# Norm with an operand in PSUM, x by transposes, two expert steps moved ahead, part of the w2 split on GpSimd

## The chip, the cores and the metric

The kernel runs on 1 core of one Trainium2 chip. The metric is the device time of one execution in microseconds (us), lower is better. Of the kernel before there are three timed runs, and one further execution was profiled.

## The reference

Two stages, one feeding the other, in float32.

```
# stage 1: mLSTM, B=2, H=8 heads, S=768 steps, D=40
m_new  = max(f[t] + m, i[t]);  fs = exp(f[t] + m - m_new);  is = exp(i[t] - m_new)
C = fs * C + is * outer(v[t], k[t]);   n = fs * n + is * k[t]
h = C @ q[t];   denom = max(|n . q[t]|, 1)
y[t] = sigmoid(o[t]) * h / denom
# stage 2: 4 experts over the 1536 tokens x = y as (1536, 320)
p = domain_probs / (domain_probs.sum(-1) + 1e-9)
out = sum_e  p[:, e] * (relu(x @ w1[e]) @ w2[e])          # w1: 320x1024, w2: 1024x320
```

## The kernel before

**Tiling.** The 1536 tokens are 12 chunks of 128 (`NCH`), six for each batch. The recurrence is turned into work on chunks: inside a chunk, scores of k and q, weighted by a decay matrix, times v; across chunks, a carried state. The expert stage works on groups: expert 0 on six groups of 256 tokens (two chunks each), experts 1 to 3 on three groups of 512. Everything is written in a fixed order (`manual_schedule`): each engine runs its instructions in the order of the program, and waits where an operand is not there.

**What is done for chunk n.** `decay(n)` is two scans on DVE (line 356). `scores(n)` is 16 matmuls into two PSUM tiles `s`, and `weigh(n)` multiplies them on DVE with the decay (line 389) into `pm`. `values(n)` and `keys(n)` scale v and k on GpSimd (lines 367, 372). `inter(n)` is the contribution of the carried state: 8 matmul instructions (line 431) and 8 scaled copies on ACT (line 438) into `yb`. `intra(n)` is 16 instructions into a PSUM tile `y0` (line 445). `state(n)` (line 398, and on DVE line 413) and `carry(n)` (GpSimd, line 419) make the next state. `norm(n)` runs on DVE (lines 454 to 466): add `yb` to `y0` into an SBUF tile `ys`, take the denominator from column 40 of each head, multiply with the gate `ogs` and with the reciprocal, and copy the last 64 channels once more behind the 320 (line 466), since the third block of x is kept twice. `turn(n)` brings x into channels by tokens: three matmuls against an identity (line 472), a copy on ACT that rounds to fp32r (line 476), and `turn_lo(n)` two subtractions on DVE (lines 481, 482) for the low halves.

**The expert stage.** An `Expert` object has steps. For a group of 256 tokens there are four `hidden` steps (16 matmuls of 256 columns each, line 128, ReLU on ACT, line 137, low half on DVE, line 138) and two `output` steps (24 matmuls of 320 columns, lines 149 to 151). A hidden step needs x of both chunks of its group. The weights are split into a high and a low part: ACT writes the high part (line 86), DVE or GpSimd subtracts (line 89). For expert 0, w1 comes in four quarters (`quarter_hi`, `quarter_lo`; hidden step i needs quarter i) and w2 in two `weights_out` calls. The raw tiles of w1 lie in the four buffers that the first four `h` tiles take afterwards.

**What sets the order around the change.** A prologue (lines 485 to 580) works out the gates of chunks 0 and 1 first and those of chunks 2 to 5 behind them (`gate_starts`, `gate_pair`, `gate_b`, `gate_i`, `gate_t`, `gate_last`, `gate_l`), and handles chunks 0 and 1. The loop at line 594 handles chunks 2 to 11, and `SLOTS` says how many expert steps go to three places of each turn of it. Chunk 0 and chunk 1 have x at the end of the prologue, and the first hidden step stands in the loop's first turn. Behind the loop the rest of expert 0 and experts 1 to 3 run.

**PSUM.** Pools `ps_h`, `ps_o`, `ps_w` and `ps_y` have two buffers each. `y0`, the inter tile, the state tile and `px` share `ps_y` in the loop.

**SP.** All DMAs are issued from SyncE in program order; line 550 writes the forget factors `fs` to DRAM, line 552 loads w2 of expert 0, and `load_f` (line 349) reads the factors back for chunks 4 and later.

Of the kernel before, what the change touches and what calls it, by code (L numbers as in the profile page):

```python
# [34 lines left out]

NPE = 4

SLOTS = ((1, 1, 1),) * 9 + ((0, 1, 1),)


@with_exitstack
def tile_mlstm_moe(ctx, tc, gt, qk, vk, ot, dp, w1, w2, out):
# [121 lines left out]
    with ExitStack() as actx:  # L164
# [80 lines left out]
        def gate_b(c0, c1):  # L245

            g = slice(c0 * L, c1 * L)
            nc.vector.tensor_tensor_scan(
                out=gat[:, 0, g], data0=fs[:, g], data1=bs[:, c0:c1].rearrange("p c t -> p (c t)"),
                initial=0.0, op0=ALU.mult, op1=ALU.add,  # L250
            )
            nc.scalar.activation(ib[32:32 + BH, g], gat[:, 0, g], AF.Copy)

        def gate_pair(c0, c1):

            g = slice(c0 * L, c1 * L)
            nc.vector.tensor_copy(fr[0:BH, g], fs[:, g])
            nc.vector.tensor_sub(fr[32:32 + BH, g], fs[:, g], fr[0:BH, g].bitcast(F32))

        pits, lasts = {}, {}  # L260

# [186 lines left out]

        def norm(n):

            y = y0s[n]
            if n % NC:
                y = a1.tile([L, H, D + 1], F32, tag="ys", name="ys")
                nc.vector.tensor_add(y, y0s[n][:, :, 0:D + 1], ybs[n])
            xr = xrs[n] = a1.tile([L, 3 * L], F32, tag=f"xr{n % 2}", name="xr")
            xh = xr[:, 0:DM].rearrange("t (h d) -> t h d", h=H)
            nq = a1.tile([L, H, 1], F32, tag="nq", name="nq")
            na = a1.tile([L, H, 1], F32, tag="na", name="na")
            nc.vector.tensor_scalar(
                out=nq, in0=y[:, :, D:D + 1], scalar1=-1.0, scalar2=1.0, op0=ALU.mult, op1=ALU.max  # L460
            )
            nc.vector.tensor_mul(xh, y[:, :, 0:D], ogs[:, n])
            nc.vector.tensor_tensor(out=na, in0=y[:, :, D:D + 1], in1=nq, op=ALU.max)
            nc.vector.reciprocal(na, na)
            nc.vector.tensor_mul(xh, xh, na.to_broadcast([L, H, D]))  # L465
            nc.vector.tensor_copy(xr[:, DM:], xr[:, DM - C:DM])

        def turn(n, pool=ps_y, tag="y"):

            px = pool.tile([L, 3, L], F32, tag=tag, name="px")  # L470
            for k in range(3):
                nc.tensor.matmul(  # L472
                    px[:, k, :], xrs[n][:, k * L:(k + 1) * L], ident, start=True, stop=True
                )
            t = slice(n * L, (n + 1) * L)
            nc.scalar.activation(xst[:, 0:3, t], px, AF.Copy)
            pxs[n] = px

        def turn_lo(n):
            px, t = pxs.pop(n), slice(n * L, (n + 1) * L)  # L480
            nc.vector.tensor_sub(xst[:, 3:5, t], px[:, 0:2], xst[:, 0:2, t].bitcast(F32))
            nc.vector.tensor_sub(xst[C:L, 2, t], px[C:L, 2], xst[C:L, 2, t].bitcast(F32))  # L482
# [34 lines left out]
        gate_f(0, 2, nc.vector)  # L517
        gate_i(0, 2, nc.vector)
        gate_starts(0, 2, nc.vector)
        gate_pair(0, 2)  # L520
        gate_b(0, 2)
        gate_max(2, NC)
        spread(0, ps_h, "ph")
# [10 lines left out]
        weigh(0)  # L534
        scores(1, ps_h, "ph")
        gate_l(0, 2)
        quarter_hi(0)
        decay(1)
        intra(0)
        state(0, ps_w, "w")  # L540
        quarter_lo(0)
        values(1)
        keys(1)
        weigh(1)
        keep_warm(256, ps_w, "w")
        inter(1, ps_w, "w")
        norm(0)
        gate_starts(2, NC, nc.vector)
        gate_pair(2, NPE)
        nc.sync.dma_start(f_d, fs)  # L550
        w2r = raws.tile([L, NF, DM], F32, tag="raw", name="w2r")
        nc.sync.dma_start(w2r, w2[0])
        gate_b(2, NC)
        gate_i(2, NC, nc.gpsimd)
        carry(1)
        intra(1)
        norm(1)
        turn(0, ps_h, "ph")
        turn_lo(0)
        spread(2, ps_o, "po")  # L560
        scores(2)
        turn(1, ps_h, "ph")
        turn_lo(1)
        quarter_hi(1)
        gate_last(2, NC)
        quarter_lo(1)
        state(1)
        gate_t(2, NC)
        gate_l(2, NC)
        decay(2)  # L570
        spread(3, ps_o, "po")
        values(2)
        keys(2)
        carry(2)
        weigh(2)
# [7 lines left out]
        work = [Expert(0, j * G, G, w1s, w2s) for j in range(NG)]

        def steps(n):
            for _ in range(n):
                if not work[0].step():
                    work.pop(0)

        def weights_out(f0):  # L590
            for f in (f0, f0 + 2):
                split_w2(w2s, f, 2, w2r, nc.vector)

        for n in range(2, NCH):
            j, cc = n // 2, n % 2
            k = SLOTS[n - 2]
            nxt = n + 1 < NCH
            if cc == 0 and j + 1 < NG:
                load_qk(j + 1)
                load_vk(j + 1)  # L600
            if NPE < n + 2 < NCH:
                load_f(n + 2)
            if cc == 0:
                gate_o(j)
                if j + 1 < NG:
                    load_o(j + 1)
            if nxt:
                decay(n + 1)
            steps(k[0])
            if n == 2:  # L610
                quarter_hi(2)
                quarter_lo(2)
            inter(n)
            if n == 3:
                weights_out(4)
            intra(n)
            state(n)
            norm(n)
            if nxt:
                scores(n + 1)  # L620
                values(n + 1)
                keys(n + 1)
                weigh(n + 1)
                carry(n + 1)
            steps(k[1])
            if n == 2:
# [118 lines left out]
```

## Time and profile before

| what | value |
|---|---|
| timed runs, median (lowest to highest) | 441.35 us (440.7 to 442.64) |
| profiled execution, its own time | 442.9 us |
| span of its trace | 441.1 us |
| mean granted clock of TensorE, share of full speed | 0.987 |
| busy: PE / DVE / ACT / GpSimd | 98% / 43% / 28% / 18% |

The share of busy time is a mean over stages that have different limits. A busy PE is not PE at its peak: matmuls overlap, so the count of instructions per microsecond and the granted clock have to be read beside it. "PEclk" is the granted clock in shares of full speed. An idle time in the timeline is given in brackets, with the engine and line whose end ended it. L with a number is a line of the kernel.

### The profile page before, as it was taken

What the parts mean: (1) busy time and instruction counts of PE and PEld (TensorE: products, weight loads), DVE (VectorE), ACT (ScalarE), POOL (GpSimd) and SP (SyncE); (2) the same over time, 40 slices, a digit from 0 to 9 for tenths busy, and PEclk for the clock granted to TensorE, in tenths of its full rate; (3) what the DMA queues carried; (4) which work ended last, traced back from release to release, by engine and by line L of the source; (5) the groups of instructions that cost most, each with busy time, mean ns of one, the idle gap of its engine ahead of it and who ended that gap; (6) DMA issues with size and microseconds to landing.
All of it is one profiled execution on the core that took longest, in us unless ns stands there. A gap on an engine that the chain in (4) does not pass through costs nothing.

```text
span 441.1 us, 6630 instructions
## 1 busy us (share of the span) xinstructions
PE 430.5 (98%) x2788; PEld 395.2 (90%) x2788; DVE 189.7 (43%) x339; ACT 125.6 (28%) x286; POOL 78.1 (18%) x88
## 2 busy tenths in 40 slices
PE   9989989999999999999999999999999999999997
PEld 5879889999999999899898898998989989889896
DVE  8985956657585622331322315223223152231321
ACT  6444523233334233420521204106022041120210
POOL 6645300112220034210430002005200010000000
PEclk9979989999999999999999999999999999999999
DMA  7992530717500003030030001100300000001001
GB/s 222 284 276 94 164 100 1 216 49 198 209 1 0 2 1 120 0 143 1 0 120 0 1 0 59 85 2 1 120 0 1 0 0 31 30 1 46 16 15 46
DMA packets 15078, 29.31 MB, mean 66 GB/s; under 512 B 1000, under 2 KB 10728, under 8 KB 13736
## 3 DMA queue, kind: packets, MB, share of 16 engines
q1 hardware_dynamic: 15048, 28.88, 20.9%
q8 instruction: 22, 0.36, 0.3%
q14 instruction: 8, 0.07, 0.0%
HBM read 26.86 MB, written 2.02 MB: 65 GB/s over the span
## 4 chain that ended last, share of the span: by engine, by line
PE 88%; DVE 10%; issue 1%; ACT 0%; DVEq 0%
PE ph L128 39%; PE po L149 13%; PE po L150 13%; PE po L151 13%; PE y L445 4%; DVE dd L356 2%; PE st L398 2%; PE s L383 2%; PE px L472 2%; PE y L431 1%; DVE xr L465 1%; DVE pm L389 1%; DVE w2s L89 1%; DVE h L138 1%; DVE cs L413 0%
## 5 line engine op out<-in xcount | busy, mean ns | idle before, releaser
L128 PE MATMUL ph<-xst,w1s 128*128 128x512 f32 (+1 forms) x960 | 185.8, 352 | 0.1
L128 PEld LDWEIGHTS ph<-xst,w1s 128*128 128x128 f32 x960 | 156.2, 191 | 25.6 <-DVE h L138 0.3
L149 PE MATMUL po<-w2s,h 128*128 128x320 f32 x384 | 120.1, 313 | 0.0
L151 PE MATMUL po<-w2s,h 128*128 128x320 f32 x384 | 119.3, 311 | 0.0
L150 PE MATMUL po<-w2s,h 128*128 128x320 f32 x384 | 119.3, 311 | 0.0
L138 DVE SCALAR_TENSOR_TENSOR h<-ph,h 128x512 fp32r<-128x512 f32 x96 | 66.3, 691 | 122.8 <-ACT h L137 122.7
L137 ACT ACTIVATE h<-ph 128x512 fp32r<-128x512 f32 x96 | 57.4, 598 | 216.4 <-PE ph L128 215.1
L149 PEld LDWEIGHTS po<-w2s,h 128*128 128x128 f32 x384 | 72.7, 189 | 0.9
L150 PEld LDWEIGHTS po<-w2s,h 128*128 128x128 f32 x384 | 72.7, 189 | 0.4
L151 PEld LDWEIGHTS po<-w2s,h 128*128 128x128 f32 x384 | 72.7, 189 | 0.0
L156 DVE SCALAR_TENSOR_TENSOR acc<-po,pw,acc 128x320 f32<-128x320 f32 x36 | 19.8, 551 | 100.0 <-PE po L151 100.0
L89 POOL TENSOR_TENSOR w1s<-raw,w1s 128x512 fp32r<-128x512 f32 (+1 forms) x24 | 23.6, 1018 | 62.0 <-ACT w1s L86 62.0
L356 DVE TENSOR_TENSOR_SCAN dd<-fb,id 128x512 f32<-128x512 f32 x24 | 28.0, 1208 | 0.2
L89 POOL TENSOR_TENSOR w2s<-raw,w2s 128x640 fp32r<-128x640 f32 x6 | 9.4, 1571 | 104.0 <-ACT w2s L86 104.0
L445 PE MATMUL y<-vp,pm 128*128 128x64 f32 x192 | 22.9, 272 | 0.6 <-DVE xst L482 0.6
L445 PEld LDWEIGHTS y<-vp,pm 128*128 128x128 f32 x192 | 22.4, 192 | 0.8 <-issue 0.7
L154 ACT ACTIVATE acc<-po,pw 128x320 f32<-128x320 f32 x12 | 6.3, 528 | 45.7 <-PE po L151 45.7
L438 ACT ACTIVATE yb<-y,ibT 128x41 f32<-128x41 f32 x80 | 16.0, 313 | 3.2 <-PE y L431 3.2
L389 DVE TENSOR_TENSOR pm<-s,dd 128x512 f32<-128x512 f32 x24 | 15.4, 684 | 0.5 <-PE s L383 0.2
L372 POOL TENSOR_TENSOR kp<-vk,dd 128x320 f32<-128x320 f32 x10 | 7.4, 738 | 43.3 <-DVE dd L356 43.3
L472 PE MATMUL px<-ident,xr 128*128 128x128 f32 x72 | 11.0, 292 | 3.5 <-DVE xr L465 3.5
L383 PE MATMUL s<-qk 64*128 64x128 f32 (+1 forms) x192 | 14.3, 285 | 0.0
(87 smaller groups left out, 241.5 us busy)
## 6 DMA issues: line engine op xcount, KB each, us to landing
raw<-in_w SPq DMA_DIRECT2D x3, 1536.0 KB, 6.2
fb<-f_d SPq DMA_DIRECT2D x8, 512.0 KB, 6.3
raw<-in_w SPq DMA_DIRECT2D x3, 1280.0 KB
qk<-in_qk SPq DMA_DIRECT2D x4, 832.0 KB
vk<-in_vk SPq DMA_DIRECT2D x4, 640.0 KB, 8.4
acc<-in_ot SPq DMA_DIRECT2D x6, 320.0 KB, 9.3
out<-acc SPq DMA_DIRECT2D x12, 160.0 KB, 1.8
qk<-in_qk SPq DMA_DIRECT2D x4, 416.0 KB
```

The lines of the kernel that those rows point to most:

```text
L89: eng.tensor_sub(lo, raw, hi.bitcast(F32))
L128: nc.tensor.matmul(ph[:, i, :], self.w1s[:, wi, f * L:(f + 1) * L], xst[:, xi, self.t0:self.t0 + n], start=(k == 0), stop=(k == len(TERMS) ...
L137: nc.scalar.activation(hh, ph, AF.Relu)
L138: nc.vector.scalar_tensor_tensor(out=hl, in0=ph, scalar=0.0, in1=hh.bitcast(F32), op0=ALU.max, op1=ALU.subtract)
L149: nc.tensor.matmul(po, hh[:, sl], ws[:, LO, f, :], start=(f == 0), stop=False)
L150: nc.tensor.matmul(po, hh[:, sl], ws[:, HI, f, :], start=False, stop=False)
L151: nc.tensor.matmul(po, hl[:, sl], ws[:, HI, f, :], start=False, stop=(f == NF - 1))
L356: nc.vector.tensor_tensor_scan(out=dds[n][:, 4 * i:4 * i + 4].rearrange("p h t -> p (h t)"), data0=fbs[n][i].rearrange("p h t -> p (h t)") ...
L383: nc.tensor.matmul(ss[n][r][:, p, :], kg[q, p], qg[q, p], start=True, stop=True)
L389: nc.vector.tensor_mul(pm[:, r], ss[n][r], dd[:, r])
L445: nc.tensor.matmul(y[:, h, :], pms[n][:, h, :], vvs[n][:, h, :], start=True, stop=True)
L472: nc.tensor.matmul(px[:, k, :], xrs[n][:, k * L:(k + 1) * L], ident, start=True, stop=True)
```

## The change

`norm(n)` writes the sum of `y0` and `yb` back into the PSUM tile `y0` and keeps the denominator and its reciprocal in spare columns of it, so that each of its operations has an operand in PSUM; the SBUF tiles `ys` and `na` and the copy of line 466 are gone. `turn(n)` uses three transposes, the third of 64 channels, and the ACT copy becomes two (the low half of the third block is subtracted from partitions 0 to 63 into 64 to 127). In the prologue, `gate_i(2, NC)` moves ahead of `decay(1)`; `gate_starts` and `gate_pair` of the later chunks go to GpSimd; quarter 0 of w1 moves behind `carry(1)`; `scores(2)` moves behind `turn(1)` and its place is taken by a `keep_warm`; `state(1)`, `gate_o(1)` and `decay(2)` move forward; and two expert steps (hidden steps 0 and 1 of group 0) stand behind x of chunk 1. `SLOTS` takes those two steps out of the loop's first turn. Quarter 3 of w1 moves ahead of `scores(3)`, and the second `weights_out` (w2 blocks 4 to 7) subtracts on GpSimd.

```diff
-SLOTS = ((1, 1, 1),) * 9 + ((0, 1, 1),)
+SLOTS = ((0, 1, 0),) + ((1, 1, 1),) * 8 + ((0, 1, 1),)
...
-        def gate_pair(c0, c1):
+        def gate_pair(c0, c1, eng):
...
-            nc.vector.tensor_copy(fr[0:BH, g], fs[:, g])
-            nc.vector.tensor_sub(fr[32:32 + BH, g], fs[:, g], fr[0:BH, g].bitcast(F32))
+            eng.tensor_copy(fr[0:BH, g], fs[:, g])
+            eng.tensor_sub(fr[32:32 + BH, g], fs[:, g], fr[0:BH, g].bitcast(F32))
...
         def norm(n):
-            y = y0s[n]
+            y, xr = y0s[n], a1.tile([L, H, D], F32, tag=f"xr{n % 2}", name="xr")
+            xrs[n] = xr.rearrange("t h d -> t (h d)")
+            yd, yn = y[:, :, 0:D], y[:, :, D:D + 1]
+            nq = a1.tile([L, H, 1], F32, tag="nq", name="nq")
+            na, ni = y[:, :, D + 2:D + 3], y[:, :, D + 4:D + 5]
             if n % NC:
-                y = a1.tile([L, H, D + 1], F32, tag="ys", name="ys")
-                nc.vector.tensor_add(y, y0s[n][:, :, 0:D + 1], ybs[n])
...
+                nc.vector.tensor_add(y[:, :, 0:D + 1], y[:, :, 0:D + 1], ybs[n])
...
-            nc.vector.tensor_mul(xh, y[:, :, 0:D], ogs[:, n])
-            nc.vector.tensor_tensor(out=na, in0=y[:, :, D:D + 1], in1=nq, op=ALU.max)
-            nc.vector.reciprocal(na, na)
-            nc.vector.tensor_mul(xh, xh, na.to_broadcast([L, H, D]))
-            nc.vector.tensor_copy(xr[:, DM:], xr[:, DM - C:DM])
+            nc.vector.tensor_mul(xr, yd, ogs[:, n])
+            nc.vector.tensor_tensor(out=na, in0=yn, in1=nq, op=ALU.max)
+            nc.vector.reciprocal(ni, na)
+            nc.vector.tensor_mul(xr, xr, ni.to_broadcast([L, H, D]))
...
         def turn(n, pool=ps_y, tag="y"):
...
-                nc.tensor.matmul(
-                    px[:, k, :], xrs[n][:, k * L:(k + 1) * L], ident, start=True, stop=True
-                )
+                r = slice(k * L, min((k + 1) * L, DM))
+                nc.tensor.transpose(px[0:r.stop - r.start, k, :], xrs[n][:, r], ident)
...
-            nc.scalar.activation(xst[:, 0:3, t], px, AF.Copy)
+            nc.scalar.activation(xst[:, 0:2, t], px[:, 0:2], AF.Copy)
+            nc.scalar.activation(xst[0:C, 2, t], px[0:C, 2], AF.Copy)
...
         def turn_lo(n):
...
-            nc.vector.tensor_sub(xst[C:L, 2, t], px[C:L, 2], xst[C:L, 2, t].bitcast(F32))
+            nc.vector.tensor_sub(xst[C:L, 2, t], px[0:C, 2], xst[0:C, 2, t].bitcast(F32))
...
         scores(1, ps_h, "ph")
         gate_l(0, 2)
-        quarter_hi(0)
+        gate_i(2, NC, nc.gpsimd)
         decay(1)
...
-        quarter_lo(0)
...
         norm(0)
-        gate_starts(2, NC, nc.vector)
-        gate_pair(2, NPE)
+        gate_starts(2, NC, nc.gpsimd)
+        gate_pair(2, NPE, nc.gpsimd)
...
+        carry(1)
+        quarter_hi(0)
+        quarter_lo(0)
         gate_b(2, NC)
-        gate_i(2, NC, nc.gpsimd)
-        carry(1)
         intra(1)
         norm(1)
         turn(0, ps_h, "ph")
         turn_lo(0)
         spread(2, ps_o, "po")
-        scores(2)
+        keep_warm(256, ps_w, "w")
         turn(1, ps_h, "ph")
         turn_lo(1)
+        scores(2)
+        state(1)
         quarter_hi(1)
         gate_last(2, NC)
         quarter_lo(1)
-        state(1)
+        gate_o(1)
+        decay(2)
+        steps(1)
         gate_t(2, NC)
+        values(2)
+        steps(1)
         gate_l(2, NC)
-        decay(2)
         spread(3, ps_o, "po")
-        values(2)
         keys(2)
...
             if n == 3:
-                weights_out(4)
+                weights_out(4, nc.gpsimd)
...
             norm(n)
+            if n == 2:
+                quarter_hi(3)
+                quarter_lo(3)
...
-            if n == 2:
-                quarter_hi(3)
-                quarter_lo(3)
...
-                weights_out(0)
+                weights_out(0, nc.vector)
```

## Rows read from the trace of the kernel before

**Rows 1.** Windows: us; PE, PEld, DVE, ACT, POOL busy (instructions); PEclk, DMA, GB/s.
```profile
75.00:100.00 25.00, 25.00 (x217) 24.59 (x217) 16.20 (x32) 7.94 (x22) 3.92 (x5) 1.00 0.42 117
```

**Rows 2.** Windows again: inside two stretches with a low granted clock.
```profile
23.50:24.00 0.50, 0.35 (x1) 0.35 (x2) 0.47 (x3) 0.00 (x0) 0.00 (x0) 0.66 0.85 348
...
58.00:59.00 1.00, 1.00 (x6) 1.00 (x5) 0.78 (x3) 0.23 (x1) 0.00 (x0) 0.50 0.01 3
```

**Rows 3.** Timeline, 16 to 24 us: start, us, engine, line, what [idle before <-releaser].
```profile
16.47 2.13 DVE L465 TENSOR_TENSOR xr<-xr,na 128x320 f32<-128x320 f32 x1
...
17.17 1.08 POOL L242 TENSOR_TENSOR ib<-gat,mb 16x512 f32<-16x512 f32 x1
...
17.74 1.60 ACT L438 ACTIVATE yb<-y,ibT 128x41 f32<-128x41 f32 x8 [1.01 <-PE y L431]
18.22 1.28 POOL L419 TENSOR_TENSOR cd<-cs,bl 104x512 f32<-104x512 f32 x1
18.64 0.91 DVE L466 COPY xr<-xr 128x64 f32<-128x64 f32 x1
...
20.54 1.21 DVE L248 TENSOR_TENSOR_SCAN gat<-fs,bs 16x512 f32<-16x512 f32 x1
20.57 0.99 PE L339 MATMUL fb<-fr,sel 48*128 48x128 f32 x7 [0.41 <-DVE fr L258]
...
23.65 1.65 PE L472 MATMUL px<-ident,xr 128*128 128x128 f32 x6 [1.03 <-DVE xr L465]
```

**Rows 4.** Timeline, 43 to 63 us: the loop's turns of chunks 2 and 3.
```profile
43.86 2.34 PE L128 MATMUL ph<-xst,w1s 128*128 128x256 f32 x16
...
50.78 0.41 PE L149 MATMUL po<-w2s,h 128*128 128x320 f32 x1
...
54.26 0.31 PE L151 MATMUL po<-w2s,h 128*128 128x320 f32 x1
...
55.20 0.68 DVE L463 TENSOR_TENSOR na<-ys,nq 128x8 f32<-128x8 f32 x1
...
56.80 0.91 PE L472 MATMUL px<-ident,xr 128*128 128x128 f32 x6 [2.23 <-DVE xr L465]
...
62.60 2.06 PE L128 MATMUL ph<-xst,w1s 128*128 128x256 f32 x16
```

**Rows 5.** Chain of waits in order of time: start, us on the chain, what.
```profile
27.57 2.35 DVE dd L356 x2
...
30.75 3.52 PE ph L128 x16
...
37.38 0.95 PE st L398 x8
38.33 1.09 PE s L383 x16
...
64.67 0.89 PE y L431 x8
65.56 1.73 PE y L445 x16
...
73.37 0.67 PE px L472 x6
74.04 1.91 PE ph L128 x16
```

**Rows 6.** Groups by line: names, count | busy us, mean ns of one | idle before.
```profile
L389 DVE TENSOR_TENSOR pm<-s,dd 128x512 f32<-128x512 f32 x24 | 15.4, 684 | 0.5 <-PE s L383 0.2
...
L89 POOL TENSOR_TENSOR w2s<-raw,w2s 128x640 fp32r<-128x640 f32 x6 | 9.4, 1571 | 104.0 <-ACT w2s L86 104.0
...
L459 DVE TENSOR_SCALAR nq<-ys 128x8 f32<-128x8 f32 x10 | 4.2, 418 | 0.3
...
L89 DVE TENSOR_TENSOR w2s<-w2r,w2s 128x640 fp32r<-128x640 f32 x4 | 3.2, 829 | 0.0
...
L459 DVE TENSOR_SCALAR nq<-y 128x8 f32<-128x8 f32 x2 | 0.3, 162 | 0.4 <-PE y L445 0.4
```

More of the change, by code (lines that the diff above doesn't have):

```diff
@@ L449, in norm @@
         def norm(n):
-            y = y0s[n]
-            if n % NC:
-                y = a1.tile([L, H, D + 1], F32, tag="ys", name="ys")
-                nc.vector.tensor_add(y, y0s[n][:, :, 0:D + 1], ybs[n])
[L455 to L458, printed above, removed]
+            y, xr = y0s[n], a1.tile([L, H, D], F32, tag=f"xr{n % 2}", name="xr")
@@ L459, in norm @@
+            xrs[n] = xr.rearrange("t h d -> t (h d)")
+            yd, yn = y[:, :, 0:D], y[:, :, D:D + 1]
+            nq = a1.tile([L, H, 1], F32, tag="nq", name="nq")
+            na, ni = y[:, :, D + 2:D + 3], y[:, :, D + 4:D + 5]
+            if n % NC:
+                nc.vector.tensor_add(y[:, :, 0:D + 1], y[:, :, 0:D + 1], ybs[n])
             nc.vector.tensor_scalar(
-                out=nq, in0=y[:, :, D:D + 1], scalar1=-1.0, scalar2=1.0, op0=ALU.mult, op1=ALU.max
+                out=nq, in0=yn, scalar1=-1.0, scalar2=1.0, op0=ALU.mult, op1=ALU.max
@@ L468, in turn @@
+            nc.vector.tensor_mul(xr, xr, ni.to_broadcast([L, H, D]))
         def turn(n, pool=ps_y, tag="y"):
-            px = pool.tile([L, 3, L], F32, tag=tag, name="px")
+            px = pxs[n] = pool.tile([L, 3, L], F32, tag=tag, name="px")
             for k in range(3):
-                nc.tensor.matmul(
-                    px[:, k, :], xrs[n][:, k * L:(k + 1) * L], ident, start=True, stop=True
-                )
+                r = slice(k * L, min((k + 1) * L, DM))
+                nc.tensor.transpose(px[0:r.stop - r.start, k, :], xrs[n][:, r], ident)
@@ L475, in turn @@
             t = slice(n * L, (n + 1) * L)
-            nc.scalar.activation(xst[:, 0:3, t], px, AF.Copy)
-            pxs[n] = px
+            nc.scalar.activation(xst[:, 0:2, t], px[:, 0:2], AF.Copy)
+            nc.scalar.activation(xst[0:C, 2, t], px[0:C, 2], AF.Copy)
         def turn_lo(n):
@@ L481, in turn_lo, with steps @@
             nc.vector.tensor_sub(xst[:, 3:5, t], px[:, 0:2], xst[:, 0:2, t].bitcast(F32))
-            nc.vector.tensor_sub(xst[C:L, 2, t], px[C:L, 2], xst[C:L, 2, t].bitcast(F32))
+            nc.vector.tensor_sub(xst[C:L, 2, t], px[0:C, 2], xst[0:C, 2, t].bitcast(F32))
+        work = [Expert(0, j * G, G, w1s, w2s) for j in range(NG)]
+        def steps(n):
+            for _ in range(n):
+                if not work[0].step():
+                    work.pop(0)
         nc.sync.dma_start(gat, gt)
@@ L519, in tile_mlstm_moe @@
         gate_starts(0, 2, nc.vector)
-        gate_pair(0, 2)
+        gate_pair(0, 2, nc.vector)
         gate_b(0, 2)
@@ L580, in tile_mlstm_moe, with weights_out @@
         load_f(NPE)
[L583 to L590, printed above, removed]
+        def weights_out(f0, eng):
             for f in (f0, f0 + 2):
-                split_w2(w2s, f, 2, w2r, nc.vector)
+                split_w2(w2s, f, 2, w2r, eng)
         for n in range(2, NCH):
@@ L603, in tile_mlstm_moe @@
             if cc == 0:
-                gate_o(j)
+                if j > 1:
+                    gate_o(j)
                 if j + 1 < NG:
```

## The prediction

> **What bounds the kernel now.** I read the table of windows first. From about 63 us on PE does nothing but stand in its own way: in 75 to 100 us it is busy all 25.00 us at the full clock, with DVE at 16.20 [rows 1]. There time is saved only by taking work off PE. Before 63 us it is otherwise. The clock column falls to half, that is from 2.4 to 1.2 GHz, between 23.5 and 24 us, and stands there at 58 to 59 us [rows 2]; between the two a hidden step that begins at 30.75 takes 3.52 us on the chain where a later one takes 1.91 [rows 5], so there too. In front of the first, PE had waited 1.03 us for DVE line 465 [rows 3]; in front of the last, 2.23 us for the same line [rows 4]. So I turned to the timeline of DVE. In chunk 0's norm, line 465 took 2.13 us and line 466 0.91 us, and under the same times stand two GpSimd operations back to back, at 17.17 for 1.08 us and at 18.22 for 1.28 us [rows 3]. The norm's operations with both operands in SBUF are the ones that stretch: line 459 takes 418 ns on the mean of ten with `ys` in SBUF, and 162 ns on both with `y` in PSUM [rows 6]. At 55.2 us line 463, an operation of the same size, takes 0.68 us [rows 4]. The chain of waits then says what a clean step costs PE: 0.89 us for inter, 1.73 for intra, 0.95 for state, 1.09 for scores, 0.67 for turn, 1.91 for a hidden step of 256 tokens, and those 3.52 for it at the low clock [rows 5]. An output step is 24 instructions between 50.78 and 54.26 us, 3.5 us [rows 4].
>
> **The change part by part.** I lay the queues of the engines side by side from 13 us on, in the new order, each operation at the duration of its row, each start at the latest of its engine and its operands. The same laying-out of the old order puts the hidden step of chunk 4 at 62.45 us, and the row says 62.60 [rows 4]; that is its accuracy.
>
> *Norm 0 and the gates.* With the operands in PSUM, line 465 costs what it costs when free, about 0.5 us for 2.13, and line 466 is gone. Norm 0 so ends near 17.05 us for 19.55, 2.5 us earlier. `gate_starts` and `gate_pair` leave DVE. On GpSimd they are four small operations of 16 partitions. The nearest row is the 16x512 subtraction at 1.08 us [rows 3], so half of it and less for each of 256 columns; I take 1.4 us for the four and bound it by 0.8 and 2.8. They end near 17.2 us, ahead of `spread(2)`, which PE reaches at 19.7. Behind them on GpSimd wait `carry(1)` and quarter 0 of w1, whose first reader is the hidden step at 24 us. Since the DRAM write of line 550 and the loads of w2 and of the factors behind it on SP now hang on GpSimd's `gate_starts`, they move from 19.8 to some 16.3 us, and nobody waits for them that early.
>
> *The scan of `gate_b`* has two SBUF operands and meets the GpSimd queue. Line 465 waited through the operations that were queued [rows 3], so I let the scan wait to the end of `carry(1)`: 18.25 to 19.45 us by the row's 1.21. This costs nothing, since norm 1 has to wait for `yb`, whose eight copies run from 17.74 for 1.60 us [rows 3], that is to 19.35. The Trainium skill, page "SBUF — State Buffer", section "SBUF: two separate sides", says that a VectorE operation with two SBUF inputs and a GpSimd operation exclude each other for a whole instruction, and which comes first blocks the other. The 2.13 us of line 465 agree, and it is the rule that speaks against handing more to GpSimd here.
>
> *Norm 1 and turn 1.* From the end of the scan at 21.75 to `px` at 23.65 norm 1 took 1.9 us [rows 3]. It now starts at 19.5 and ends at 21.5, 2.1 us earlier. The sum in place is written to PSUM, and three operations write there; no row shows such a write. Reading PSUM costs nothing by line 459 (162 ns for a like operation), so I take zero, with +0.06 us for each of the norm's operations as the upper bound (about a third of such a row), which moves the end of the critical stretch by 0.7 us. A gain is excluded, since the operands are as many. With `scores(2)` behind it, PE reaches turn 1 at about 21.0 (turn 0, `spread(2)` and the added `keep_warm` of 0.45 us) and waits 0.6 us instead of 1.03. A wait of 0.41 us at 20.57 was followed by no fall of the clock, one of 1.03 us was [rows 3], so I expect none here.
>
> *The transposes.* A turn is six instructions of 0.67 us now, two for each float32 matmul [rows 5]. No row shows a transpose. If each is one such instruction, a turn costs 0.34. The cheapest instruction of 128 columns in the chain is that of the scores, 1.09 us for 16, which gives 0.20 for three; no gain at all would be 0.67. I take 0.35, the count halved, which is the nearest in kind, and keep the ends. The Trainium skill, page "TensorE: Matmul & The Clock Gate", section "Terms", calls the transpose mode four times faster for float32; by it a turn costs 0.17 us and the sum below is 2.2 us lower. No run here shows it yet. ACT's second copy, about 0.25 us more, lies beside PE work in the loop.
>
> *From turn 1 to hidden step 3.* PE's list from 21.55 us is: turn 0.35, scores 1.09, state 0.95, hidden 1.91, `gate_t` (eight small instructions at the 0.11 us of a turn's) 0.9, hidden 1.91, `gate_l` 0.2, `spread(3)` 0.9, inter 0.89, together 9.1, so 30.7 us. Then it waits for `weigh(2)`, which stands on DVE behind `decay(2)` (2.35 us from about 24.9) and behind the low half of the second hidden step (ReLU done 29.55, low half 30.3); two operations of 0.68 us [rows 6] end it near 31.5. That is the new wait, 0.8 us. Intra 1.73, state 0.95, scores 1.09, hidden 1.91, turn 0.35 and hidden 1.91 follow without a gap, 7.95 us, to 39.5. Before, this hidden step ended at about 46.0 [rows 4]. The 6.5 us are the two waits, the two low-clock stretches (1.6 us each by 3.52 against 1.91) and the shorter turns; the two hidden steps fill time in which PE waited. Quarters 0 and 1 are split on GpSimd by 25.3 us, just ahead of hidden step 0's ReLU, which takes over their buffer.
>
> *Chunk 3.* DVE loses two subtractions of 0.83 us, the stretch of lines 459 and 463 (0.68 for some 0.16, so about 1.0 us for the two) and the copy. Laid out: half of w2 and the probabilities to 42.2, `decay(4)` to 44.5, low half, state, norm 3 to 47.85. PE from 39.5: inter, intra, state, scores with 0.4 us of waits to 44.6, output step 3.5 to 48.1, then turn 3. So PE no longer waits 2.23 us, but DVE is only 0.3 us ahead. GpSimd's two subtractions take 1.57 us each [rows 6] and end at 46.4, ahead of their readers (blocks 4 and 5 at 46.4, 6 and 7 at 47.3), with no slack either. Turn 3 and the second output step end at 52.0; the row of before is 62.60. That is 10.6 us.
>
> *The loop behind it.* Eight more turns (chunks 4 to 11) save 0.32 us each, 2.6 us, all on PE, which is the bound there. Sum: 13.2 us off.
>
> **The rivals.** (a) *The clock falls once more.* The wait of 0.8 us for `weigh(2)` lies between the waits that kept the clock and the 1.03 us that did not. A fall costs 1.6 us, since PE is the bound behind it: 11.6 off, 430 to 431. (b) *GpSimd becomes the bound of the prologue.* If the scan waits until quarter 0 is done (21.9 us), norm 1 ends at 25.1, PE idles four microseconds, the clock falls, and the hidden step of chunk 4 comes at 57.2 for 52.0: 8 off, 434. Against it: line 465 waited for two operations, not four. (c) *The gain isn't there:* the steps moved ahead are stalled by their weights or buffers (quarter 1, the `h` buffers) and wait as they would have in the loop, and the transposes cost what the matmuls did: 439 to 442. Against it, the quarters are split 2 us earlier than before. (d) *Slower: the clock falls at each turn.* If the 0.3 us of transposes, joined to the small waits beside them, work on the clock as idle time does, each of the ten turns in the loop is followed by a low stretch worth 1.6 us: 16 on and 13.2 off, with the two stretches saved in the prologue lost again (3.2), about 447. It decides once nine of the ten fall so. The rows speak against it: a wait of 0.41 us did nothing. The Trainium skill's page "TensorE: Matmul & The Clock Gate", section "Part 4: PE-mode transpose", says that transposes do not count as activity for the clock; by it this rival is real, and no run here shows it yet.
>
> **How the numbers follow.** The profiled execution took 442.9 us, 1.8 over its span and 1.55 over the median of 441.35; 442.9 less 13.2 is 429.7, and against the median 428.2. The slacks of 0.8, 0.3 and 0 us can only lose, so I put 1.3 us back: 429.5. The low end takes 0.20 us for a turn (12 times 0.15, 1.8 us less) from 428.2, and leaves 0.9 us for what a freer DVE gives the loop: 425.5. The high end takes two falls of the clock (3.3 us), the PSUM writes (0.7), turns no cheaper than now (4), less what overlaps: 436, which takes in (a) and (b). Chances: forecast 0.55, (a) 0.2, (b) 0.15, (c) 0.06, (d) 0.04. Half of (c) lies within 0.5%, about the least that a measurement of this kernel tells from no change; so faster 0.92, within 0.03, slower 0.05 with some for what I don't see.
>
> **What would show it.** Right: line 465 near 0.5 us in every norm; `px` of chunk 1 near 21.5 us with under 0.7 us of wait; no low clock between 20 and 62 us; the hidden step of chunk 4 near 52 us; a turn at 0.35 us or less in the chain. Wrong: a wait in front of turn 1 or of intra 2 over 1 us with a low clock behind it; the scan of line 248 stretched past 20 us; output step 0 waiting for GpSimd's w2; px in three instructions that take as long as six.

## The result, and the profile after

The changed kernel takes 431.01 us (median of 4 runs, 430.58 to 431.67) against 441.69 (440.7 to 442.64) of the kernel before beside it: ratio 0.976, 95% interval 0.9733 to 0.9787. The forecast was 429.5, in a range of 425.5 to 436. The profiled execution took 431.67 us with a span of 428.8, 12.3 us under the 441.1 of before.

The windows first, with the columns of [rows 1]. The stretch of 75 to 100 us, where PE was the bound, is unchanged: PE is busy 24.99 of 25.00 us. What is new stands in the other two rows: the clock column is 1.00 from 13 to 60 us, and in 58 to 59 us too, where [rows 2] has 0.50.

```profile
13.00:60.00 47.00, 45.43 (x388) 42.22 (x387) 36.52 (x70) 24.04 (x73) 26.49 (x31) 1.00 0.72 203
75.00:100.00 25.00, 24.99 (x215) 24.44 (x214) 16.25 (x31) 7.53 (x23) 4.92 (x6) 1.00 0.50 138
...
58.00:59.00 1.00, 1.00 (x13) 0.90 (x14) 0.25 (x1) 0.00 (x0) 0.00 (x0) 1.00 0.00 0
```

The timeline of 15 to 24 us, the answer to [rows 3]. Line 464 (line 465 before) takes 0.49 us for 2.13 in norm 0; the four gate operations on GpSimd run from 15.69 to 17.28; PE waits 0.26 us in front of turn 1, at 21.38 for 23.65.

```profile
15.69 0.18 POOL L237 COPY bs<-fs 16x4 f32<-16x4 f32 x1
...
16.56 0.72 POOL L258 TENSOR_TENSOR fr<-fs,fr 16x256 fp32r<-16x256 f32 x1
16.62 0.49 DVE L464 TENSOR_TENSOR xr<-xr,y 128x320 f32<-128x320 f32 x1
17.03 1.33 DVE L248 TENSOR_TENSOR_SCAN gat<-fs,bs 16x512 f32<-16x512 f32 x1
...
17.36 1.84 POOL L419 TENSOR_TENSOR cd<-cs,bl 104x512 f32<-104x512 f32 x1
...
19.24 0.51 DVE L457 TENSOR_TENSOR y<-y,yb 128x328 f32<-128x328 f32 x1 [0.88 <-PE y L445]
...
20.84 0.49 DVE L464 TENSOR_TENSOR xr<-xr,y 128x320 f32<-128x320 f32 x1
...
21.38 0.55 PE L471 MATMUL px<-ident,xr 128*128 128x128 f32 x3 [0.26 <-DVE xr L464]
```

Further on in the timeline, up to the step that [rows 4] has at 62.60: the first moved hidden step at 23.70; intra 2, whose first head starts at 31.27 and whose other weight loads (PEld) wait 0.18 us for the second operation of `weigh(2)`; hidden step 3 at 37.59; and the hidden step of chunk 4 at 53.00. Between them, at 41.94 and 42.98, stand two groups that are longer than alone (2.34 and 3.14 us), and behind them the largest wait that PE has left.

```profile
23.70 2.15 PE L128 MATMUL ph<-xst,w1s 128*128 128x256 f32 x16
...
30.31 1.28 DVE L389 TENSOR_TENSOR pm<-s,dd 128x512 f32<-128x512 f32 x2
...
31.27 2.15 PE L445 MATMUL y<-vp,pm 128*128 128x64 f32 x16
...
31.64 1.64 PEld L445 LDWEIGHTS y<-vp,pm 128*128 128x128 f32 x14 [0.18 <-DVE pm L389]
```
```profile
37.59 2.15 PE L128 MATMUL ph<-xst,w1s 128*128 128x256 f32 x16
...
41.94 3.67 DVE L356 TENSOR_TENSOR_SCAN dd<-fb,id 128x512 f32<-128x512 f32 x2
...
42.98 3.98 POOL L89 TENSOR_TENSOR w2s<-w2r,w2s 128x640 fp32r<-128x640 f32 x2 [4.98 <-ACT w2s L86]
...
48.48 0.49 DVE L464 TENSOR_TENSOR xr<-xr,y 128x320 f32<-128x320 f32 x1
...
49.11 0.52 PE L471 MATMUL px<-ident,xr 128*128 128x128 f32 x3 [0.94 <-DVE xr L464]
...
53.00 2.06 PE L128 MATMUL ph<-xst,w1s 128*128 128x256 f32 x16
```

In the chain of waits a turn is now three instructions of 0.33 us together; [rows 5] has six of 0.67.

```profile
63.76 0.33 PE px L471 x3
64.09 1.91 PE ph L128 x16
```

The span divides at the hidden step of chunk 4. Ahead of it 62.60 became 53.00, 9.6 us less; behind it 441.1 - 62.60 = 378.5 became 428.8 - 53.00 = 375.8, 2.7 less for eight turns of 0.34.

### The profile page after: what moved, and what is told of

The parts are those of the page before. It is cut to its first block, busy times and chain, and to the rows that moved or that the text cites. A ratio compares the mean times of both kernels' runs of the same rounds, so it can differ in the third digit from the quotient of the medians.

```text
span 428.8 us, 6587 instructions
## 1 busy us (share of the span) xinstructions
PE 421.1 (98%) x2754; PEld 386.2 (90%) x2754; DVE 180.1 (42%) x321; ACT 125.7 (29%) x298; POOL 82.3 (19%) x94
## 4 chain that ended last, share of the span: by engine, by line
PE 91%; DVE 4%; DMA 2%; issue 1%; ACT 1%; SPq 0%; POOL 0%; DVEq 0%
PE ph L128 41%; PE po L149 13%; PE po L150 13%; PE po L151 13%; PE y L445 5%; PE s L383 2%; PE y L431 2%; PE st L398 2%; DMA acc<-in_ot 2%; PE px L471 1%; DVE y L457 0%; DVE xr L461 0%; DVE w2s L89 0%; DVE xr L464 0%; DVE dd L356 0%
## 5 line engine op out<-in xcount | busy, mean ns | idle before, releaser
L356 DVE TENSOR_TENSOR_SCAN dd<-fb,id 128x512 f32<-128x512 f32 x24 | 29.3, 1264 | 0.2
L383 PEld LDWEIGHTS s<-qk 64*128 64x128 f32 (+1 forms) x192 | 11.8, 187 | 1.9 <-DVE dd L356 0.8
```

The lines of the kernel that those rows point to most:

```text
L356: nc.vector.tensor_tensor_scan(out=dds[n][:, 4 * i:4 * i + 4].rearrange("p h t -> p (h t)"), data0=fbs[n][i].rearrange("p h t -> p (h t)") ...
L383: nc.tensor.matmul(ss[n][r][:, p, :], kg[q, p], qg[q, p], start=True, stop=True)
```

## The experiments

One table serves all of them. For each kernel's profiled execution it gives the start of chunk 4's hidden step (timeline), PE's idle time from 13 us to it (the stretch less PE's busy time in the windows), the low clock in it (summed over windows of half a microsecond), the span, and the rest of the span behind that step. A microsecond at the low clock costs half a microsecond of a full engine, so start less idle less half the low clock is what PE's work alone needs. This comes to 49.5 to 53.4 us in all thirteen; what moves the step by ten is mostly idle time and clock. The rows of before and after from which the first two columns come, in this order:

```profile
13.00:62.60 49.60, 43.98 (x333) 41.59 (x333) 40.02 (x76) 20.30 (x58) 20.37 (x24) 0.90 0.62 180
```
```profile
13.00:53.00 40.00, 38.43 (x323) 35.55 (x321) 34.28 (x66) 20.59 (x61) 25.77 (x30) 1.00 0.80 225
```

| kernel | step at | idle | low clock | span | behind |
|---|---|---|---|---|---|
| before | 62.60 | 5.6 | 10.2 | 441.1 | 378.5 |
| after | 53.00 | 1.6 | 0 | 428.8 | 375.8 |
| u1_again: after, turn by matmul, third block 64 | 53.73 | 0.4 | 0 | 434.4 | 380.7 |
| u6: after, turn by matmul, third block 128 | 52.88 | 0.4 | 0 | 431.2 | 378.3 |
| p4: before, transposes alone | 61.04 | 6.0 | 10.2 | 437.3 | 376.3 |
| u2: after, norm with its sums in SBUF | 59.45 | 5.9 | 3.4 | 435.7 | 376.3 |
| p1: before, norm alone, third block 64 | 59.48 | 5.0 | 3.4 | 440.2 | 380.7 |
| p3: before, norm alone, third block 128 | 58.27 | 4.8 | 3.4 | 436.7 | 378.4 |
| p2: before, norm and transposes | 57.61 | 4.7 | 6.8 | 433.4 | 375.8 |
| u3: after, the two steps back in the loop | 56.62 | 2.4 | 6.8 | 432.5 | 375.9 |
| u5: after, no keep-warm ahead of turn 1 | 56.11 | 2.2 | 6.8 | 432.9 | 376.8 |
| u4: after, all of w2 on DVE | 53.27 | 1.9 | 0 | 429.1 | 375.8 |
| b1: a step further, below | 52.27 | 0.6 | 0 | 426.4 | 374.1 |

The theory was that of the prediction: the gain is mostly time that PE idles or runs at the low clock before chunk 4, freed by the norm and the new order together, and 0.3 us a turn behind it. The rivals were that one part carries it all, and that the order or the work on GpSimd adds nothing. Of the order, the two steps and the `keep_warm` were undone one at a time; the other moves (the gates on GpSimd, `gate_i`, quarters 0 and 3, `scores(2)`) were not.

### The turn

u1_matmul_turn puts the float32 matmuls back into the changed kernel, with a third block of 64 channels:

```diff
-                nc.tensor.transpose(px[0:r.stop - r.start, k, :], xrs[n][:, r], ident)
+                nc.tensor.matmul(
+                    px[0:r.stop - r.start, k, :], xrs[n][:, r], ident, start=True, stop=True
+                )
```

> The changed kernel with one part undone: x is brought over by three float32 matmuls against the identity again (two instructions each), not by transposes; the third stays at 64 channels. Theory (PE is the bound from the fourth chunk on, and a turn is three instructions of 0.33 us there where it was six of 0.67): the eight turns of chunks 4 to 11 cost 0.34 us more each, 2.7 us, and the four turns before them up to 1.3 us more; span 428.8 + 2.7 to 4.0 = 431.5 to 432.8. A turn of 0.67 us in the chain. Rival (the turns lie beside other work, or a transpose is only a shorter name for the same time): under 1 us, span below 429.8.

Measured: 436.22 us, ratio to before 0.9874 (0.9847 to 0.9901), 5.2 over the changed kernel where 2.7 to 4.0 were expected. So this was no clean undoing; u1_again is the same kernel, for a trace of it.

> The same kernel as the first experiment (x by float32 matmuls, not transposes), to have a profile at the full clock: its timed spans were 434.4 us, 5.6 over the changed kernel, where the count of turns gave 4.0 at most. Theory: each of the twelve turns costs 0.34 us more on PE (4.1 us), and the rest, 1.5 us, is one wait that grows in chunks 1 to 3, where DVE's chain begins with a turn: turn 1 and turn 3 wait for line 464 longer than 0.26 and 0.94 us. Rival: no wait grows, and a turn by matmuls costs 0.8 us or more in place of 0.67.

Measured: 436.2 us, span 434.4: the rival. No wait grew (0.4 us of idle time in the table). The chain shows the turn itself and the step behind it longer:

```profile
64.49 0.81 PE px L471 x6
65.30 2.10 PE ph L128 x16
```

0.81 + 2.10 is 0.67 us over the 0.33 + 1.91 of after, and 0.33 over the 0.67 + 1.91 of before [rows 5]. The block of 64 channels was the suspect, so u6_matmul_turn_128 takes 128 channels in all three, as the kernel before did, and reads the upper half of the third:

```diff
-                r = slice(k * L, min((k + 1) * L, DM))
-                nc.tensor.transpose(px[0:r.stop - r.start, k, :], xrs[n][:, r], ident)
+                w = xrs[n][:, k * L:(k + 1) * L] if k < 2 else xrs[n][:, DM - L:DM]
+                nc.tensor.matmul(px[:, k, :], w, ident, start=True, stop=True)
 ...
-            nc.scalar.activation(xst[0:C, 2, t], px[0:C, 2], AF.Copy)
+            nc.scalar.activation(xst[0:C, 2, t], px[C:L, 2], AF.Copy)
 ...
-            nc.vector.tensor_sub(xst[C:L, 2, t], px[0:C, 2], xst[0:C, 2, t].bitcast(F32))
+            nc.vector.tensor_sub(xst[C:L, 2, t], px[C:L, 2], xst[0:C, 2, t].bitcast(F32))
```

> The changed kernel with the turn as float32 matmuls of three times 128 channels (channels 192 to 319 in the third), as the kernel before had them. Theory: the run with 64 channels in the third lost 0.3 us a turn to that block alone, so here a turn takes 0.59 to 0.67 us from its first instruction to the next step, as in the kernel before, and nothing else moves: 8 x 0.34 = 2.7 us behind chunk 4 and up to 0.7 for turns 0 to 3, a span of 431.5 to 432.3. Rival: float32 matmuls in this turn cost 0.9 us whatever the block, because of what stands behind them, and the span is the 434.4 of that run.

Measured: span 431.2, 0.3 us under the theory's band and far from the rival's 434.4, and the chain has the turn of before:

```profile
63.64 0.67 PE px L471 x6
64.31 1.92 PE ph L128 x16
```

So the transposes are worth 378.3 - 375.8 = 2.5 us behind chunk 4. Ahead of it they are worth nothing here: the step starts at 52.88 for 53.00, since the longer turns lie in time that PE idles otherwise (0.4 for 1.6 us). These are figures of profiled executions. The median of u6 is 434.54 (433.06 to 437.53; ratio 0.9851, 0.9791 to 0.9911), because two of its four runs had a mean clock of 0.992 and 0.988 and spans of 434.2 and 435.8, the other two 0.999 and 1.0 and 431.2 and 431.3. All four runs of the changed kernel had 428.8. Why the mean clock is lower in some runs of u6 and in none of after, no trace here shows.

p4_turn_only gives the kernel before the turn of the changed one and drops the copy of doubled channels, nothing else.

> The kernel before with nothing but the transposes (no doubled channels, no copy of them), norm as before. Theory: 0.34 us for each of the turns of the loop that PE bounds (8 to 10), and the copy of 0.91 us gone from norm 0; the low clock stays: a span of 437.3 to 438.5. Rival: with the copy gone PE's wait before turn 1 falls under the length that the clock stands, the first low stretch goes too, and the span is 435.5 to 436.7.

Measured: 439.21 us, ratio 0.9951 (0.9933 to 0.997), span 437.3, the lower end of the theory's band. The low clock is as long as before, 10.2 us, but not in the same places. PE waits 1.03 us ahead of turn 1, as before, and this time the clock stays at 1.00 behind it; a stretch of 6.8 us begins at 28.2 us instead. The wait in front of turn 3 is still there, with the fall around it. The two turns in the timeline, and the windows at turn 1 with the columns of [rows 1]:

```profile
22.91 0.55 PE L472 MATMUL px<-ident,xr 128*128 128x128 f32 x3 [1.03 <-DVE xr L465]
...
55.73 0.87 PE L472 MATMUL px<-ident,xr 128*128 128x128 f32 x3 [2.20 <-DVE xr L465]
```
```profile
22.00:23.00 1.00, 0.09 (x1) 0.10 (x2) 0.93 (x5) 0.75 (x3) 0.00 (x0) 1.00 1.01 420
23.00:24.00 1.00, 1.00 (x11) 1.00 (x11) 0.49 (x2) 0.51 (x3) 0.00 (x0) 1.00 0.96 399
```

### The norm

u2_norm_sbuf writes the norm's sum, its denominator and the reciprocal to SBUF again:

```diff
-            na, ni = y[:, :, D + 2:D + 3], y[:, :, D + 4:D + 5]
+            na = a1.tile([L, H, 1], F32, tag="na", name="na")
+            ni = na
 ...
-                nc.vector.tensor_add(y[:, :, 0:D + 1], y[:, :, 0:D + 1], ybs[n])
+                ys = a1.tile([L, H, D + 1], F32, tag="ys", name="ys")
+                nc.vector.tensor_add(ys, y[:, :, 0:D + 1], ybs[n])
+                yd, yn = ys[:, :, 0:D], ys[:, :, D:D + 1]
```

> The changed kernel with one part undone: the norm's sum and its denominator lie in SBUF again (no second copy of the channels, though). Theory (operations of DVE with two operands in SBUF, or copies in SBUF, wait for GpSimd's operations, and it is that which made the norms late): the last product of norm 0 stretches from 0.5 us to 1.0 or more, the scan of gate_b behind it and the operations of norm 1 meet the split of quarter 0 on GpSimd, turn 1 comes 1 to 2 us later, PE waits there over 1 us and the clock may fall (1.6 us); in chunk 3 the norm meets w2's subtractions again, about 1 us. Together 2 to 5 us: span 431 to 434. Rival (the order of the steps alone brought the gain): within 0.7 us of 428.8.

Measured: 437.72 us, ratio 0.9902 (0.9866 to 0.9939), 6.7 us over the changed kernel and more than expected. The timeline of DVE and of GpSimd, norm 2, where u2's line numbers are three higher than those of the changed kernel: its line 464, the product with the gate (line 461 of the changed kernel, 0.48 us there), now has two operands in SBUF and takes 2.04 us, beside two GpSimd operations back to back, which themselves take what they take elsewhere (0.72 to 0.74 and 1.03 to 1.04 us).

```profile
39.02 0.77 DVE L461 TENSOR_SCALAR nq<-ys 128x8 f32<-128x8 f32 x1
39.70 2.04 DVE L464 TENSOR_TENSOR xr<-ys,acc 128x320 f32<-128x320 f32 x1
```
```profile
39.66 0.74 POOL L372 TENSOR_TENSOR kp<-vk,dd 128x320 f32<-128x320 f32 x1
40.35 1.04 POOL L419 TENSOR_TENSOR cd<-cs,bl 104x512 f32<-104x512 f32 x1
```

PE waits 1.62, 1.96 and 1.99 us in front of turns 1, 2 and 3, where the changed kernel waits 0.26, nothing and 0.94. Idle time (5.9 us) is back at the level of before.

p1_norm_only is the other direction: the kernel before with the norm in PSUM alone, the copy of line 466 gone with it. Its turn by matmul had the third block of 64.

> The kernel before with one part alone: the norm with an operand in PSUM, without the second copy of the channels; x still by matmuls, the order as before. Theory (DVE's waits for GpSimd in the norms made the late turns): norm 0 ends 2.5 us earlier, turn 1 no longer makes PE wait 1.03 us, the low clock at 23.7 us is gone; the hidden step of chunk 2 starts near 27.5 us for 30.7; turn 3 waits 1 us for 2.23. Span 441.1 less 5 to 8 = 433 to 436. Rival (without the new order another wait of DVE's, the scans of decay 2, takes the place at once): 438 or more.

Measured: 442.22 us, ratio 0.9999 (0.9982 to 1.0015), span 440.2: a miss, in the rival's band. PE's wait in front of turn 1 did not go away either (1.17 us for 1.03), though the clock stayed up behind it. p3_norm_only_128 takes the price of that block out, with the turn of u6.

> The kernel before with nothing but the norm's operands in PSUM; the turn as float32 matmuls of three times 128 channels, order as before. Theory: the run of the norm alone that showed no gain carried 0.3 us a turn from its block of 64 channels, 12 x 0.3 = 3.6 us; without that the span is 436.4 to 437.6, 3.5 to 4.7 under the kernel before. Rival: the norm alone gives nothing as long as the old order leaves the low clock around 30 us and the waits before px: 439.5 to 441.

Measured: 439.36 us, ratio 0.9954 (0.9937 to 0.9971), span 436.7 (436.6 to 438.5 in ten runs). The profiled execution and five other runs are in the theory's band, the other four 0.7 to 0.9 us above it. So the block had hidden the gain: 440.2 - 436.7 = 3.5 us for 12 turns. Of the 4.3 us that the step of chunk 4 comes earlier, 3.4 are half of the 6.8 us by which the low clock is shorter, and 0.8 idle time. By the other runs (mean clock 0.988 to 0.996) that part varies from run to run.

p2_norm_turn_only has norm and transposes in the old order.

> The kernel before with the norm in PSUM and the transposes, and the order as before: what the new order is worth is this less the changed kernel. Theory: the transposes take 12 times 0.34 = 4 us from the kernel with the norm alone, as in the changed kernel; span 429.5 to 432.5, so the order with the two moved steps is worth 1 to 4 us of the 12.3. Rival (the order carries most of it): 434 or more.

Measured: 436.69 us, ratio 0.9876 (0.9848 to 0.9903), span 433.4 in the profiled execution, 0.9 us over the theory's band, and 434.8 to 434.9 in the other three, which is the rival's. So the new order is worth 4.6 to 6.1 us of span, not 1 to 4: between a third and a half of the 12.3. Behind chunk 4 it is the changed kernel (375.8). Ahead of it the old order still idles 4.7 us and runs 6.8 us at the low clock.

### The order

u3_steps_in_loop puts the two hidden steps back into the loop:

```diff
-SLOTS = ((0, 1, 0),) + ((1, 1, 1),) * 8 + ((0, 1, 1),)
+SLOTS = ((1, 1, 1),) * 9 + ((0, 1, 1),)
 ...
-        steps(1)
         gate_t(2, NC)
         values(2)
-        steps(1)
```

> The changed kernel with one part undone: the first two hidden steps stand in the loop's turn of chunk 2 again, everything else stays where the change put it. Theory (they filled time in which PE waited for DVE): PE waits some 2 us between gate_t and spread 3 for decay 2, and the clock falls to half for about 3.3 us behind that; the 3.8 us of the two steps come back in the loop, less what waits there anyhow: 3 to 5.5 us more, span 432 to 434.3. Rival (DVE is the bound through chunks 2 and 3, so that it doesn't matter where PE does them): under 1 us more.

Measured: 434.62 us, ratio 0.9833 (0.98 to 0.9866), as expected, 3.6 over the changed kernel. The two steps were filling, though the price came by another way than expected: without them PE idles only 0.8 us more where 2 were expected, but the clock falls at 25.9 us and stays low until 32.7, twice as long as expected.

u5_no_keep_warm drops the one `keep_warm(256, ps_w, "w")` that the change puts ahead of turn 1.

> The changed kernel without the keep-warm matmul that it puts ahead of turn 1. PE's wait of 0.26 us there then grows by its 0.45 or more, to 0.7 to 1.0 us. Theory: that stays under the 1.03 us after which the clock fell before, nothing falls, and the span is 428.6 to 429.2. Rival: the clock falls behind turn 1 and the span is 430.4 to 431.2 (1.6 us for a hidden step at the low clock, and more for what lies beside it).

Measured: 434.56 us, ratio 0.9842 (0.9806 to 0.9877), 3.6 over the changed kernel: the rival, and twice its price. PE's timeline at turns 1 and 3, and the windows from 20 us:

```profile
21.64 0.90 PE L471 MATMUL px<-ident,xr 128*128 128x128 f32 x3 [0.88 <-DVE xr L464]
```
```profile
52.23 0.52 PE L471 MATMUL px<-ident,xr 128*128 128x128 f32 x3 [0.94 <-DVE xr L464]
```
```profile
20.00:21.00 1.00, 0.76 (x7) 0.62 (x6) 0.90 (x5) 0.96 (x3) 1.00 (x1) 1.00 1.00 348
21.00:21.50 0.50, 0.00 (x0) 0.00 (x0) 0.47 (x2) 0.31 (x2) 0.50 (x2) 0.64 1.16 430
...
22.00:26.00 4.00, 4.00 (x28) 3.39 (x26) 0.93 (x3) 3.38 (x6) 2.00 (x3) 0.50 0.85 341
```

The wait grows from 0.26 to 0.88 us, and within it the clock falls to half, 1.2 GHz, and stays there for 6.8 us, through turn 1, the scores, the state and most of a hidden step. Turn 1 starts 0.26 us later than in the changed kernel, turn 3 3.1 us later. The last microsecond of the 4.1 between the spans comes with a second low stretch, of 3.4 us at 144 us, behind a wait of 0.91 us ahead of intra 11. The changed kernel has that wait as well and no fall behind it; what the `keep_warm` at 20 us has to do with this stretch isn't shown. The wait of 0.94 us ahead of turn 3 is longer than that of 0.88 and is followed by no fall, here as in the changed kernel. So 0.70 us of matmuls on zeros, as the timeline of the changed kernel has them at 20.43, are worth 3.1 us by turn 3, and 3.6 us by the medians.

### The part of w2 on GpSimd

u4_w2_dve is one word:

```diff
-                weights_out(4, nc.gpsimd)
+                weights_out(4, nc.vector)
```

> The changed kernel with one part undone: the second half of w2 is subtracted on DVE again. Theory from the trace of the changed kernel (the two subtractions on GpSimd took 3.98 us for 3.14 and the scans of decay 4 at their side 3.67 for 2.34, so that moving 1.66 us off DVE gave 1.33 us back): DVE ends norm 3 some 0.3 us later, the wait of 0.94 us in front of turn 3 grows to about 1.3; span 428.8 + 0.3 = 429.1, between 428.7 and 429.8 if the clock stays. Rival (the working of the prediction: the move frees DVE by its full 1.66 us): turn 3 comes 1.7 us later, PE waits 2.6 us and the clock falls: span 430.5 to 432.2.

Measured: 431.28 us, ratio 0.9764 (0.9739 to 0.9788), span 429.1 for 428.8. The move is worth 0.3 us. The timeline of DVE and PE: the scans of decay take 2.33 us for 3.67 once GpSimd's subtractions are away, and DVE pays 1.74 us for doing them itself, so norm 3 ends 0.3 us later.

```profile
41.89 2.33 DVE L356 TENSOR_TENSOR_SCAN dd<-fb,id 128x512 f32<-128x512 f32 x2
...
44.72 1.74 DVE L89 TENSOR_TENSOR w2s<-w2r,w2s 128x640 fp32r<-128x640 f32 x2
...
49.40 0.52 PE L471 MATMUL px<-ident,xr 128*128 128x128 f32 x3 [1.32 <-DVE xr L464]
```

### A version that beats both

The waits that PE has left in the changed kernel are 0.94 us ahead of turn 3, 0.91 ahead of intra 11 and 0.36 ahead of turn 11. b1_probs_slots moves DVE's four operations on the probabilities (lines 641 to 644) from the loop into the prologue, behind `values(2)`, where DVE has time, and lets the last pair of chunks have all its slots:

```diff
-SLOTS = ((0, 1, 0),) + ((1, 1, 1),) * 8 + ((0, 1, 1),)
+SLOTS = ((0, 1, 0),) + ((1, 1, 1),) * 9
 ...
```

> The changed kernel with two of its remaining waits of PE attacked: the four DVE operations of the probabilities stand in the prologue ahead of the second hidden step, where DVE waits 2 us, instead of between w2 and decay 4; and the loop's last turn has an expert step in its first place too, ahead of intra 11. Theory: the wait of 0.94 us in front of turn 3 goes to 0.1 to 0.3, and the one of 0.91 us in front of intra 11 goes; span 428.8 - 1.4 to 1.8 = 427.0 to 427.4. Rival (the wait in front of turn 3 is made by decay 4 meeting GpSimd's subtractions, and stays; the waits of chunk 11 come back behind its turn): 428.3 to 428.8.

Measured: 427.91 us (427.67 to 430.74, 6 runs), ratio 0.969 (0.9664 to 0.9717), span 426.4, 0.6 us under the theory's band. The waits of PE (engine, line, what it waited for: us in total, times, longest) that are left:

```profile
PE pwm L67 <- PEq L727: 0.8, 1, 0.8
PE y L431 <- ACT cs L74: 0.3, 1, 0.3
PE px L471 <- DMA w2r<-in_w: 0.2, 1, 0.2
```

All three waits are gone, 0.7 us ahead of chunk 4 and 1.7 behind it. The scans of decay 4 now run from 41.58 to 43.91 us and GpSimd's subtractions from 43.44, so that they overlap for only 0.5 us (2.33 us, and 3.35 for those on GpSimd). The two edits were not run apart; that the first gives the 0.7 and the second the 1.7 goes by where the waits lay.

## Why the prediction was right, step by step

The mechanism held. Of the 9.6 us ahead of chunk 4, 4.0 are idle time (5.6 to 1.6) and 5.1 are the clock (half of 10.2 us); 0.5 is less work. No single part carries this. Alone, the norm is worth 2.0 us by the medians and the transposes 2.2, each with the copy of line 466 gone; together in the old order 5.9 (442.61 of before in that comparison less 436.69), and the changed kernel 10.7. By the profiled spans the first three are 4.4, 3.8 and 7.7, so that up to there they nearly add. Taken out of the changed kernel one by one, the norm costs 6.7, the two steps 3.6, the keep-warm 3.6, the transposes 2.4 by the spans, together 16.3. These don't add up to 10.7, and the table shows one reason: without the two steps or without the keep-warm, the same 6.8 us of low clock come back. Rivals (a) to (c) did not come: the clock did not fall in any of the four runs (mean 0.999 to 1.0), norm 1 ended at 21.33 us and not at 25.1, and the moved steps started at 23.70 and 26.80 with no wait in front.

*Norm 0 and the gates.* Forecast: norm 0 to 17.05 us, the gates 1.4 us of GpSimd and ended at 17.2. They ended at 17.11 and at 17.28, and the four took 1.38 us (0.18, 0.09, 0.39 and 0.72).

*Writes to PSUM.* Taken as zero, with 0.06 us an operation as the bound. The groups by line say that zero was nearest: line 457, the sum in place, takes 508 ns (line 454 of before, into SBUF, 496), line 458 has the 162 ns of [rows 6] nearly to the digit. That operation (line 459 before) reads one tensor, not two, so its 418 ns for 166 also say that not only work with two inputs in SBUF was held up.

```profile
L457 DVE TENSOR_TENSOR y<-y,yb 128x328 f32<-128x328 f32 x10 | 5.1, 508 | 3.3 <-PE y L445 3.1
...
L458 DVE TENSOR_SCALAR nq<-y 128x8 f32<-128x8 f32 x12 | 2.0, 166 | 0.8 <-PE y L445 0.4
```

*The scan of gate_b.* I let it wait for `carry(1)`, to 19.45 us. It was the other way round: the scan began first, at 17.03, took 1.33 us, and `carry(1)`, which began 0.33 us later, took 1.84 for 1.28 in [rows 3]. The Trainium skill, page "SBUF — State Buffer", section "SBUF: two separate sides", has the one that comes first block the other, and this trace agrees on which of the two waited; I had not asked which came first. It cost nothing, as norm 1 waited for other things.

*Turn 1.* Forecast 21.5 us with a wait of 0.6 and no fall; it is 21.38, with 0.26, and no fall. The argument behind it, that a fall hangs on the length of the wait, between 0.41 and 1.03 us, is wrong: u5 falls in a wait of 0.88, the changed kernel doesn't after 0.94, and p4 waits the same 1.03 us ahead of the same turn as before without a fall. So that none came here was partly luck: the `keep_warm`, which the forecast counted as 0.45 us of PE's list and nothing else, is what it hung on by u5.

*The transposes.* 0.35 us was taken and 0.33 is in the chain, for the reason given: one instruction each for two. The estimate from the Trainium skill's page "TensorE: Matmul & The Clock Gate", section "Terms", was 0.17 us; the trace doesn't bear it out. Nor did rival (d) come, for which I had named the Trainium skill's page "TensorE: Matmul & The Clock Gate", section "Part 4: PE-mode transpose": no turn of the loop is followed by a low clock, and the windows from 13 to 60 us have 1.00. Whether transposes count as activity is neither shown nor refuted by this, for the three last 0.3 us together.

*To hidden step 3.* Forecast to end at 39.5; the next step starts at 39.58. The bound was where the forecast had it: `weigh(2)` ended at 31.59 for 31.5, and intra 2 could not go on before (its first head alone began at 31.27). What was wrong is PE's own list up to there, 9.9 us (21.38 to 31.27) for 9.1. It took up the forecast wait of 0.8 us, of which 0.18 is left, and so cost nothing.

*Chunk 3.* The missing microsecond is here: 53.00 for 52.0. I freed DVE of two subtractions of 0.83 us and counted that as its gain. The scans of decay 4 and those subtractions, now on GpSimd, ran into each other, 3.67 us for 2.34 and 3.98 for 3.14. DVE lost 1.33 of the 1.66 us again, which is the 0.3 that u4 measures, and norm 3 ended at 48.97 for 47.85, with PE waiting 0.94 us. The scans of decay 4 have both operands in SBUF, and that such work of DVE is held up by GpSimd's, as line 465 was in [rows 3], was not put into the sum where it mattered.

*The loop.* 2.6 forecast, 2.7 measured, 2.5 by u6.

*The sum and its base.* 13.2 us forecast and 12.3 measured, of one profiled execution to another: 442.9 - 12.3 = 430.6. The other 0.4 us to the median of 431.01 lie outside the span. In the forecast I took off the 1.55 us between that execution and the median, and put 1.3 back. The 1.55 should have stayed. Among the runs of before beside the experiments, a mean clock of 0.991 to 0.992 goes with spans of 438.7 to 440.3, and 0.983 to 0.988 with 440.0 to 441.7: the shorter ones already had less of the low clock that the change takes away. That is worked out from those pairs and was not traced.

*The price of a fall.* Rival (a) had 1.6 us. The three low stretches of before (23.7 to 27.1, 30.5 to 33.9 and 57.8 to 61.2) cost about that, 3.4 us at half speed each. The one of u5 lasted 6.8 us and cost 3.1 by turn 3.

## What to carry to other kernels

Where a clock falls around short waits, lay the waits of several runs side by side and count what each costs with the low stretch behind it, instead of reading a limit from two of them: 0.7 us of work on zeros was worth 3.1 us and more. An operation that leaves a busy engine hasn't left it if it then runs beside that engine's work with two operands in SBUF and stretches it. When a part is undone to price it, keep the shape of what was there before: a block of 64 channels made the price of the norm vanish (0.9999 with it, 0.9954 without).

## What the runs showed of the hardware that was not expected

- The third float32 matmul with 64 channels is dearer than with 128. Beside u6 the turn of u1_again takes 0.14 us more and the step behind it 0.18 more, and over all turns 434.4 - 431.2 = 3.2 us; p1 against p3 says 3.5. The third transpose of the changed kernel is as narrow and shows no such price (0.33, then 1.91). What the engine does there, the profile doesn't say.
- A longer wait can leave the clock where it is. In u2 PE is busy 1.04 of 3.00 us and in p3 0.15 of 1.50, both at a granted clock of 1.00, ahead of turns 2 and 3; ahead of turn 1 of u5, 0.88 us was enough for 0.50. Nor is it the place: ahead of the same turn 1, p4, p2 and p1 wait 1.03, 1.08 and 1.17 us with no fall until 28.2, 24.7 and 29.2 us. Two windows, of u2 and then of p3:

```profile
40.00:43.00 3.00, 1.04 (x10) 0.87 (x9) 2.93 (x5) 0.60 (x1) 1.39 (x2) 1.00 0.01 3
```
```profile
52.50:54.00 1.50, 0.15 (x2) 0.02 (x1) 1.40 (x5) 0.53 (x1) 1.11 (x2) 1.00 1.08 317
```

  What sets these cases apart stays open.
- DVE and GpSimd stretch each other in both directions: in these rows the one that starts second is the longer (`carry(1)` at 17.36 behind the scan at 17.03; line 464 of u2 at 39.70 behind an operation of 39.66), and where each has two operations in a row, both stretch, as from 41.9 to 47 us.
